# The last two token blocks of a first layer: seven products replaced by plain steps, and the second layer's weight conversion spread over the steps

## The chip, the cores and the metric

The kernel runs on one core of a Trainium2 chip. The metric is the device time of one execution in microseconds. The engines have queues of their own that work in order: PE multiplies matrices, ACT (ScalarE) and DVE (VectorE) work elementwise, POOL (GpSimd) too, and SP issues nearly all DMA transfers. The traces put all operations that go through the kernel's ordering helper on its line 62, so rows are told apart by tile names.

## The reference, cut to what matters

Chunked attention (4 batches, 8 heads, 768 positions, 64 per head, 8 memory keys) gives 3072 tokens of 512 values. Two layers follow:

```python
h = x @ w_in                                  # 3072 x 512 @ 512 x 2048
g = np.maximum(h, 0.0) + np.log1p(np.exp(-np.abs(h)))     # first layer: softplus
y = g @ w_out                                 # 2048 x 512
h = y @ w_in2
g = np.maximum(h, 0.0) + alpha * np.minimum(h, 0.0)       # second layer
out = g @ w_out2
```

Each fp32 operand is split into a high and a low part that PE can multiply at full speed, and a product of two operands is three matmuls: high by high, high by low, low by high.

## The kernel before

**Tokens and hidden units.** The tokens are 6 blocks of 512 (`NB`), the hidden units 16 strips of 128 (`NF`). A plain step (`pe_h` L408, `act_first` L421, `high`/`low` L429 and L434, `pe_out` L469) takes one block and one strip: 12 matmuls of 128x512 from the resident weights `W[f]` into a PSUM bank (`ps_hh`), softplus and split on ACT and DVE (`ta`, `g`), and 12 matmuls into the four sums of the block (`ps_o`). `SEGMENTS` (L43) lists the steps: blocks 0 and 1 in alternating pieces, then blocks 2 and 3 whole, 64 steps (`NPLAIN` = 4).

**Pairs.** Blocks 4 and 5 of the first layer, and all six of the second, go through in pairs with fewer multiplications: `quad` (L575) computes two strips for both blocks of a pair by seven products of 6 matmuls each (`ps_q`), where steps would take 48 matmuls in the same place, from seven combinations of the weights and seven of the activations. Eight quads make a pair, and `pairs` (L637) runs them and then the rest of the output sums. The first product of a quad is copied by ACT (`tc<-ps_q`). `PAIRS` (L45) is one pair of the first layer, then three of the second. A pair's operands are streamed from DRAM: `in_ops` holds the weight combinations in eight groups (one for each quad), `out_ops` the output weights, each already split. The activations come from `y_dram`, and for the first layer's pair from `x_dram`, to which attention stores blocks 4 and 5 (`a_high` L375).

**Weights.** The inputs arrive as float64 words. `load_raw` (L170) loads 128x512 of them, `convert_a` and `convert_b` (L176, L191) turn them into fp32 with five DVE instructions (`word`), and for the second layer each group of four such halves then takes: the sums on POOL (`weight_sums` L232, tile `wsum`), and six stagings, each a high part cast by ACT (`high_to`, `wst`), a low part subtracted by POOL and a store issued by SP (`low_to` L224). The raw words, the sums and the stagings share three buffers (`raw` in the plan), the words two.

**Order.** Before anything is issued, `Plan.run` (L91) walks through the pieces that `add` registered (engine, reckoned us, due time, what they come after, buffers taken and given) and writes them out in the order in which they would start; that is then the order of every in-order queue. Pieces without an engine stand for transfers, with a reckoned duration. Attention's 24 tiles are pieces of this plan with due times between the steps. The sums of the first layer's weights (L754) come first; behind the last of them (`before`, L776) the second layer's conversion begins, with five of the eight groups in the plan (`EARLY`, L775) and three in a list `rest` that `quad` takes piece by piece through `fill` (L613, L618, L625). What remains of `rest` runs at the end of the first pair's quads (L649).

**The seam.** `switch_pools` (L484) gives attention's buffers to the activations of the pairs, `load_y`, `sum_y` and `split_y` make the operands of the first pair, and buffers of `W` become free as the last block's steps finish (`w` in the plan). The last output sums of the steps are issued inside the first quad.

Of the kernel before, what the change touches and what calls it, by code (L numbers as in the profile page):

```python
# [135 lines left out]
def attention_mlp_mlp_kernel(ctx: ExitStack, tc, qk, v, w1, w2, consts, out):  # L136
# [26 lines left out]
    x_dram = dpool.tile([DM, NTOK - NPLAIN * N2], F32, name="x_dram")  # L163
    in_ops = [dpool.tile([NQ, P, 2, 7, HK], F32, name=f"in_ops{n}") for n in range(2)]
    out_ops = [dpool.tile([NQ, P, 2, 2, DM], F32, name=f"out_ops{n}") for n in range(2)]
# [62 lines left out]
    def split_to(src, n, to):  # L228

        low_to(src, n, high_to(src, n), to)  # L230

    def weight_sums(layer, q):  # L232
        if layer:
            m0, m1 = words[1, 4 * q], words[1, 4 * q + 2]
        else:
            m = rpool.tile([P, 2, DM], F32, tag="raw", name="wboth")
            for e in range(2):
                w = W[2 * q + e].bitcast(F32)
                nc.gpsimd.tensor_tensor(out=m[:, e, :], in0=w[:, 0, :DM], in1=w[:, 1, :DM], op=ALU.add)
            m0, m1 = m[:, 0, :], m[:, 1, :]  # L240
        t = rpool.tile([P, 4, HK], F32, tag="raw", name="wsum")
# [5 lines left out]
        sums[layer, q] = t  # L247

    def split_sums(layer, q, n):
        split_to(sums[layer, q][:, n:n + 2, :], DM, in_ops[layer][q][:, :, S1 + n:S1 + n + 2, :])  # L250
        if n:
            sums.pop((layer, q))

    def store_plain(q):

        for e in range(2):
            w = W[2 * q + e].bitcast(F32)
            if e == 0:
                nc.sync.dma_start(out=in_ops[0][q][:, :, A11:A12 + 1, :], in_=w[:, :, :DM].rearrange("p a (k n) -> p a k n", k=2))
            else:  # L260
                nc.sync.dma_start(out=in_ops[0][q][:, :, A22, :], in_=w[:, :, HK:DM])
            nc.sync.dma_start(out=out_ops[0][q][:, e], in_=w[:, :, DM:])

    def split_plain(q):
        split_to(words.pop((1, 4 * q)), DM, in_ops[1][q][:, :, A11:A12 + 1, :])
        split_to(words.pop((1, 4 * q + 2))[:, HK:], HK, in_ops[1][q][:, :, A22, :])

    def split_out(f):
        split_to(words.pop((1, 2 * f + 1)), DM, out_ops[1][f // 2][:, f % 2])
# [105 lines left out]
    def a_high(t):  # L375
        room, (b, c) = st[t][0], divmod(t, TB)
        if b < NPLAIN:
            n = slice(c * QT, (c + 1) * QT)
            for e, x in enumerate(x_of(b)):
                act.copy(out=x[:, 0, :, n], in_=x_ps[t][:, 2 * e:2 * e + 2, :])  # L380
        else:
# [109 lines left out]
    def load_y(p, h):  # L491

        layer, pair = PAIRS[p]
        src, first = (y_dram, 0) if layer else (x_dram, NPLAIN)
        for key, kc, b in ((B11, h, 0), (T1, h, 1), (B21, h + 2, 0), (B22, h + 2, 1)):
            t = y_raw[p, h, key] = raw_y("yraw")
            tok = (2 * pair + b - first) * N2
            nc.sync.dma_start(out=t, in_=src[kc * P:(kc + 1) * P, tok:tok + N2])
# [27 lines left out]
    def load_w_in(n):  # L526
        if n >= len(PAIRS) * NQ:
            return
        p, q = divmod(n, NQ)
        for a, b in ((0, 4), (4, 7)):  # L530
            t = wpool.tile([P, 2, b - a, HK], F32R, tag="w", name="win")
            nc.sync.dma_start(out=t.bitcast(F32), in_=in_ops[PAIRS[p][0]][q][:, :, a:b, :])
# [3 lines left out]
    def load_w_out(n):  # L536
        if n >= 2 * len(PAIRS) * NQ:
# [3 lines left out]
        nc.sync.dma_start(out=t.bitcast(F32), in_=out_ops[PAIRS[p][0]][q % NQ])  # L541
# [13 lines left out]
    def activate(layer, src, f, to):  # L555
        if not layer:
            act.activation(out=to, in_=src, func=AF.Softplus)
            return
# [4 lines left out]
    def out2(p, b, f):  # L563
        n = (2 * p + b) * NQ + f // 2
        layer, pair = PAIRS[p]
        if f == 0:
            acc[p, b] = acc_banks()
        out_sums(acc[p, b], layer, g2.pop((p, b, f)), w_out[n][:, f % 2], f == 0, f == NF - 1)
# [3 lines left out]
        if f == NF - 1:  # L572
            drain(acc.pop((p, b)), layer, 2 * pair + b)

    def quad(p, q, between, fill):  # L575
        n, layer = p * NQ + q, PAIRS[p][0]
# [29 lines left out]
        activate(layer, x1, f0, a0)  # L606
# [6 lines left out]
        fill()  # L613
        product(p, n, A22, T4, x3, False)
        activate(layer, stash[p, f1], f1, stash[p, f1])
        a1 = tpool.tile([P, N2], F32, tag="ta", name="ta", bufs=2)
        activate(layer, x3, f1, a1)
        fill()  # L618
# [18 lines left out]
    def pairs(between, rest):  # L637
        def fill():
            if rest:
                rest.pop(0)()  # L640

        for p in range(len(PAIRS)):
            for q in range(NQ):
                quad(p, q, between, fill)
# [4 lines left out]
            while rest:  # L649
                fill()  # L650
# [58 lines left out]

    def tile(t, prev, due):  # L710
# [10 lines left out]
        for u in range(2):  # L721
            add(("s", t, u), "PE", 0.5, due - 13, lambda u=u: a_scores(t, u), [("qk", t)] + ([("s", t, 0)] if u else [("s", prev, 1)] if prev >= 0 else []) + ([("m", t - 2, u)] if start and t > 1 else [("t", TB - 1, 1)] if t == TB else []),
# [8 lines left out]
        to_dram = t >= NPLAIN * TB  # L731
        for u in range(2):
            add(("t", t, u), "PE", 0.45, due - 5, lambda u=u: a_transpose(t, u), [("n", t)], ["pa"], ["s"] if u and few and not to_dram else [])
            add(("pt", t, u), "ACT", 0.58, due - 4, lambda u=u: a_turned(t, u), [("t", t, u)], [("tb", "tl")[u]], ["pa"])
        free_x = {2: [("ds", 23)], 3: [("ds", 31)]}.get(t // TB, [])
        add(("v*", t), "PE", 0.9, due - 3, lambda: a_values(t), [("pt", t, 0), ("pt", t, 1), ("v", t)], ["h" if start else "pa"], ["tb", "tl"] + (["v"] if few else []))
        if to_dram:
            add(("xh", t), "ACT", 0.6, due - 2, lambda: a_high(t), [("v*", t)], [], ["pa"])
            add(("xl", t), "", 4.0, due, lambda: None, [("xh", t)], [], ["s"])
        else:  # L740
            add(("xh", t), "ACT", 0.75, due - 2, lambda: a_high(t), [("v*", t)] + free_x)
            add(("xl", t), "DVE", 0.84, due - 1, lambda: a_low(t), [("xh", t)], [], ["h" if start else "pa"])
# [11 lines left out]
    for q in range(NQ):  # L754
        due = when[23 + 15 * q // 8] + 20
        add(("sums", q), "POOL", 6.6, due, lambda q=q: (store_plain(q), weight_sums(0, q)),
            [("wl", 4 * q + k) for k in range(4)] + [("raw", 2 * NF - 1)] + ([("sl", q - 1, 2)] if q else []), ["raw", "raw"], ["raw"])
        for n in (0, 2):
            def high_piece(q=q, n=n):
                staged[q, n] = high_to(sums[0, q][:, n:n + 2, :], DM)  # L760

            def low_piece(q=q, n=n):
                low_to(sums[0, q][:, n:n + 2, :], DM, staged.pop((q, n)), in_ops[0][q][:, :, S1 + n:S1 + n + 2, :])
            add(("sh", q, n), "ACT", 0.62, due + 3 * n, high_piece, [("sums", q)], ["raw"])
            add(("sl", q, n), "POOL", 1.6, due + 3 * n, low_piece, [("sh", q, n)], [], ["raw"] if n else [])
            add(("ss", q, n), "", 5.0, 0, lambda: None, [("sl", q, n)], [], ["raw"])

    halves = [4 * q + k for q in range(NQ) for k in (0, 2, 1, 3)]

    def weights2(j):  # L770
        convert(1, halves[j])
        if j + 1 < len(halves):
            load_raw(1, halves[j + 1])

    EARLY = 5  # L775
    before = [("sl", NQ - 1, 2)]  # L776
# [136 lines left out]
```

## Time and profile before

| | |
|---|---|
| Median of 3 runs (lowest, highest) | 1256.76 us (1253.38, 1258.38) |
| The profiled execution | 1255.99 us, span of its instructions 1254.2 us |
| PE busy | 1130.6 us, 5760 matmuls |
| DVE, ACT, POOL busy | 735.4, 437.2, 190.6 us |
| Mean granted clock of PE | 0.956 |
| DMA | 263.96 MB, mean 210 GB/s |

The span runs from the first to the last instruction; the execution's own time adds what lies around it. Busy shares are averages over stages with different limits, so the stages are to be read apart: attention start-up (to about 80 us), steps with attention (to 494 us), the first layer's pair (to 758 us), the second layer. The clock is the mean of what was granted to PE, 1.00 being 2.4 GHz and 0.50 being 1.2 GHz.

### The profile page before, as it was taken

To read this page: it belongs to the slowest core of one execution; us is meant where nothing else is said; L and a number is where in the kernel's file an instruction comes from. 1 tells how busy PE (TensorE), PEld (TensorE's weight loads), DVE (VectorE), ACT (ScalarE), POOL (GpSimd) and SP (SyncE) were. 2 spreads that over 40 slices of the span, in tenths; PEclk is the share of its full clock that TensorE was granted. 3 is DMA by queue.
4 is the path that set the end of the run, shared out by engine and by line. 5 is a ranking of instruction groups with operands and counts; after the bars stand their busy time and mean duration, and the time that the engine had idled before them with its cause. 6 is when DMAs were issued, how large, how long until landed. Compare 5 with 4: busy or idle time off the path is not lost.

```text
span 1254.2 us, 15594 instructions
## 1 busy us (share of the span) xinstructions
PE 1130.6 (90%) x5760; PEld 934.4 (74%) x5760; DVE 735.4 (59%) x1488; ACT 437.2 (35%) x810; POOL 190.6 (15%) x180
## 2 busy tenths in 40 slices
PE   6889989999999996054987799999999999999998
PEld 5778878888888785044865588888888888888887
DVE  5889878544567565323552555666656666665542
ACT  5775454554535333122232242111421113311122
POOL 0011214655322213312211100000000000000000
PEclk9999999999999998577998799999999999999999
DMA  9967975645545576473867666446765457554450
GB/s 303 291 221 248 277 226 180 190 118 159 185 138 211 182 269 238 155 241 120 306 241 270 243 227 226 170 172 246 272 245 195 152 196 287 194 225 166 174 225 34
DMA packets 84316, 263.96 MB, mean 210 GB/s; under 512 B 7056, under 2 KB 15248, under 8 KB 76048
## 3 DMA queue, kind: packets, MB, share of 16 engines
q1 hardware_dynamic: 81936, 258.77, 58.6%
q0 software_dynamic: 2304, 4.20, 2.2%
q8 instruction: 45, 0.74, 0.2%
q14 instruction: 31, 0.25, 0.1%
HBM read 197.93 MB, written 65.01 MB: 210 GB/s over the span
## 4 chain that ended last, share of the span: by engine, by line
PE 72%; DMA 13%; DVE 7%; ACT 3%; POOL 2%; issue 2%; SPq 1%; ACTq 0%; DVEq 0%; POOLq 0%
PE ps_o L62 35%; PE ps_q L62 21%; PE ps_hh L62 10%; DMA raw<-in_w_dram 5%; DMA in_ops<-wst 4%; DVE word L62 3%; PE ps_s L62 3%; PE ps_x L62 2%; POOL wst L225 2%; PE ps_t L62 2%; DMA x_dram<-s_sb 1%; DVE s_sb L62 1%; DMA out_ops<-wst 1%; ACT wst L62 1%; DMA y_dram<-o_sb 1%
## 5 line engine op out<-in xcount | busy, mean ns | idle before, releaser
L62 PE MATMUL ps_q<-xop,win 128*128 128x512 f32 x1344 | 325.8, 398 | 83.0 <-ACT tc L62 79.8
L62 PEld LDWEIGHTS ps_q<-xop,win 128*128 128x128 f32 x1344 | 257.9, 192 | 140.2 <-ACT tc L62 81.7
L62 PE MATMUL ps_o<-wout,g 128*128 128x512 f32 x1152 | 268.8, 389 | 0.0
L62 PEld LDWEIGHTS ps_o<-wout,g 128*128 128x128 f32 x1152 | 216.2, 188 | 44.9
L62 PE MATMUL ps_o<-g,wsplit 128*128 128x512 f32 x768 | 191.9, 400 | 5.9 <-DVE g L62 3.6
L62 PE MATMUL ps_hh<-x,wsplit 128*128 128x512 f32 x768 | 189.5, 396 | 1.6 <-ACT x L62 1.2
L62 PEld LDWEIGHTS ps_o<-g,wsplit 128*128 128x128 f32 x768 | 145.0, 192 | 37.3 <-DVE g L62 4.5
L62 PEld LDWEIGHTS ps_hh<-x,wsplit 128*128 128x128 f32 x768 | 143.2, 190 | 31.9 <-ACT x L62 1.4
L62 DVE TENSOR_TENSOR g<-ta,g 128x512 fp32r<-128x512 f32 x128 | 102.3, 799 | 72.8 <-ACT g L62 69.2
L62 ACT CAST g<-ta 128x512 fp32r<-128x512 f32 x128 | 79.6, 622 | 110.8 <-DVE ta L62 105.8
L62 ACT COPY tc<-ps_q 128x512 f32<-128x512 f32 x64 | 37.6, 587 | 210.3 <-PE ps_q L62 204.2
L62 PE MATMUL ps_o<-g,wout 128*128 128x512 f32 x384 | 92.4, 396 | 3.7 <-ACT o_sb L62 2.8
L62 DVE SCALAR_TENSOR_TENSOR word<-raw,word 128x512 int32<-128x512 int32 x128 | 92.7, 725 | 3.8
L62 DVE TENSOR_TENSOR g<-gb,g 128x512 fp32r<-128x512 f32 x64 | 45.0, 703 | 77.4 <-ACT g L62 76.9
L62 PEld LDWEIGHTS ps_o<-g,wout 128*128 128x128 f32 x384 | 73.7, 192 | 20.3 <-ACT o_sb L62 3.2
L62 DVE TENSOR_TENSOR u<-ps_q,tc 128x512 f32<-128x512 f32 x32 | 22.1, 691 | 94.0 <-PE ps_q L62 69.1
L62 ACT CAST g<-gb 128x512 fp32r<-128x512 f32 x64 | 39.9, 623 | 102.4 <-PE ps_o L62 102.2
L62 ACT ACTIVATE ta<-ps_hh 128x512 f32<-128x512 f32 x64 | 38.3, 598 | 95.0 <-PE ps_hh L62 94.9
L62 DVE TENSOR_SCALAR word<-raw 128x512 int32<-128x512 int32 x64 | 34.4, 538 | 55.9 <-DMA raw<-in_w_dram 35.7
L62 PE MATMUL ps_s<-qk 128*128 128x96 f32 x384 | 53.9, 295 | 10.9 <-DMA qk<-in_qk_dram 6.1
L62 DVE TENSOR_SCALAR word<-word 128x512 f32<-128x512 f32 (+1 forms) x128 | 60.5, 473 | 4.4
L62 PEld LDWEIGHTS ps_s<-qk 128*128 128x128 f32 x384 | 52.2, 210 | 13.6 <-DMA qk<-in_qk_dram 6.4
(62 smaller groups left out, 994.1 us busy)
## 6 DMA issues: line engine op xcount, KB each, us to landing
wout<-out_ops SPq DMA_DIRECT2D x64, 1024.0 KB, 7.1
raw<-in_w_dram SPq DMA_DIRECT2D x64, 512.0 KB, 5.3
win<-in_ops SPq DMA_DIRECT2D x32, 1024.0 KB, 7.0
win<-in_ops SPq DMA_DIRECT2D x32, 768.0 KB, 7.0
in_ops<-wst SPq DMA_DIRECT2D x40, 512.0 KB, 3.2
qk<-in_qk_dram SPq DMA_DIRECT2D x24, 832.0 KB, 6.2
v<-in_v_dram SPq DMA_DIRECT2D x24, 384.0 KB, 5.6
out_ops<-wsplit SPq DMA_DIRECT2D x16, 512.0 KB, 3.9
```

What stands on the lines that cost most here:

```text
L62: i = getattr(self.engine, name)(*args, **kw)
L225: nc.gpsimd.tensor_tensor(out=t[:, 1, :n], in0=src, in1=t[:, 0, :n].bitcast(F32), op=ALU.subtract)
```

## The change

All six blocks of the first layer become plain steps (96 of them), so the first layer's pair goes, with `x_dram`, the first layer's `in_ops` and `out_ops`, the sums of its weights and their stores; `activate` becomes `prelu` on DVE alone. Attention writes the x operand of blocks 2 to 5 into the buffers of blocks that are finished two blocks earlier (`drained`). The second layer's conversion has all eight groups in the plan, begins behind the first layer's last raw load, has due times over steps 24 to 86, and `rest` and `fill` go. The plan's reckoned times change for some pieces: raw loads of the second layer 8 us (5 before), staged stores 6 (5), and attention's work on PE. The operands of the first pair are due by the last steps of the longer list, and the removed functions (`split_sums`, `store_plain`, `split_plain`, `split_out`, `weights2`) have no caller left.

```diff
-NPLAIN = 4
-SEGMENTS = [(b, f0, f1) for f0, f1 in ((0, HALF // 2), (HALF // 2, HALF), (HALF, NF)) for b in range(2)] + [(b, 0, NF) for b in range(2, NPLAIN)]
-PAIRS = [(0, p) for p in range(NPLAIN // 2, NB // 2)] + [(1, p) for p in range(NB // 2)]
+SEGMENTS = [(b, f0, f1) for f0, f1 in ((0, HALF // 2), (HALF // 2, HALF), (HALF, NF)) for b in range(2)] + [(b, 0, NF) for b in range(2, NB)]
+NPAIRS = NB // 2
...
     def a_high(t):
-        room, (b, c) = st[t][0], divmod(t, TB)
-        if b < NPLAIN:
-            n = slice(c * QT, (c + 1) * QT)
-            for e, x in enumerate(x_of(b)):
-                act.copy(out=x[:, 0, :, n], in_=x_ps[t][:, 2 * e:2 * e + 2, :])
-        else:
-            o = room[:, :DM].rearrange("p (k n) -> p k n", k=KD)
-            act.copy(out=o, in_=x_ps.pop(t))
-            tok = t * QT - NPLAIN * N2
-            nc.sync.dma_start(out=x_dram.rearrange("(k p) n -> p k n", p=P)[:, :, tok:tok + QT], in_=o)
+        b, c = divmod(t, TB)
+        n = slice(c * QT, (c + 1) * QT)
+        for e, x in enumerate(x_of(b)):
+            act.copy(out=x[:, 0, :, n], in_=x_ps[t][:, 2 * e:2 * e + 2, :])
...
+    drained = [max(i for i in range(len(steps)) if steps[i][0] == b) for b in range(NB)]
...
-        free_x = {2: [("ds", 23)], 3: [("ds", 31)]}.get(t // TB, [])
+        free_x = [("ds", drained[t // TB - 2])] if t >= 2 * TB else []
...
-        + [(16 + c, when[9 + 3 * c] + 10) for c in range(TB)] + [(8 + c, when[22 + 2 * c] + 10) for c in range(TB)]
-        + [(12 + c, when[31 + 3 * c] + 10) for c in range(TB)] + [(20 + c, when[43 + 3 * c] + 10) for c in range(TB)]
+        + [(TB * b + c, when[drained[b - 2] - 2 + (2 if b == 2 else 3) * c] + 10) for b in range(2, NB) for c in range(TB)]
...
-    EARLY = 5
-    before = [("sl", NQ - 1, 2)]
-    add(("raw2", 0), "", 5.0, 0, lambda: load_raw(1, halves[0]), before, ["raw"])
-    for j in range(4 * EARLY):
+    add(("raw2", 0), "", 8.0, 0, lambda: load_raw(1, halves[0]), [("raw", 2 * NF - 1)], ["raw"])
+    for j in range(4 * NQ):
         q, e = divmod(j, 4)
-        k, due = halves[j], when[33 + 28 * j // (4 * EARLY)]
-        add(("cv2", j), "DVE", 2.75, due, lambda j=j: convert(1, halves[j]), [("raw2", j)] + ([("cv2", j - 1)] if j else []), ["word"], ["raw"])
-        add(("raw2", j + 1), "", 5.0, 0, lambda j=j: load_raw(1, halves[j + 1]), [("cv2", j)] + ([("sh2", q - 1, 1, 1)] if 0 else []), ["raw"])
+        k, due = halves[j], when[24 + 64 * j // (4 * NQ)]
+        add(("ca2", j), "DVE", 1.35, due, lambda j=j: convert_a(1, halves[j]), [("raw2", j)] + ([("cv2", j - 1)] if j else []), ["word"])
+        add(("cv2", j), "DVE", 1.42, due, lambda j=j: convert_b(1, halves[j]), [("ca2", j)], [], ["raw"])
+        if j + 1 < 4 * NQ:
+            add(("raw2", j + 1), "", 8.0, 0, lambda j=j: load_raw(1, halves[j + 1]), [("cv2", j)], ["raw"])
...
-            add(("ss2",) + name, "", 5.0, 0, lambda: None, [("sl2",) + name], [], ["raw"])
+            add(("ss2",) + name, "", 6.0, 0, lambda: None, [("sl2",) + name], [], ["raw"])
...
-        due = when[55 + 4 * h]
+        due = when[last - 8 + 4 * h]
...
-    pairs(lambda: pe_out(last), rest)
+    pairs(lambda: pe_out(last))
```

## Rows read from the trace of the kernel before

**Rows 1.** The page, engine totals: busy us, share of the span, instructions.
```profile
PE 1130.6 (90%) x5760; PEld 934.4 (74%) x5760; DVE 735.4 (59%) x1488; ACT 437.2 (35%) x810; POOL 190.6 (15%) x180
```

**Rows 2.** Stages: stretch, length, PE, PEld, DVE, ACT, POOL busy, clock, DMA share, GB/s.
```profile
80.00:331.00 251.00, 246.00 (x1519) 204.57 (x1520) 173.67 (x414) 130.89 (x204) 99.83 (x92) 0.99 0.66 202
331.00:468.00 137.00, 134.25 (x769) 111.24 (x769) 86.75 (x199) 60.82 (x95) 28.13 (x28) 0.99 0.58 202
468.00:494.00 26.00, 20.10 (x77) 15.55 (x76) 15.66 (x22) 10.08 (x18) 7.78 (x7) 0.87 0.75 274
494.00:758.00 264.00, 177.35 (x723) 142.68 (x722) 114.61 (x180) 71.41 (x127) 48.36 (x47) 0.83 0.64 225
758.00:921.00 163.00, 163.00 (x721) 134.97 (x720) 99.39 (x154) 38.13 (x66) 0.00 (x0) 1.00 0.60 219
```

**Rows 3.** Waits of PE from 468 to 758 us: total us, times, longest.
```profile
PE ps_q L62 <- ACT tc L62: 79.8, 4, 48.6
```

**Rows 4.** Timeline of PE about the seam: start, us, operation, idle before it.
```profile
473.82 0.50 PE L62 MATMUL ps_o<-g,wsplit 128*128 128x512 f32 x1 [2.35 <-ACT g L62]
477.07 5.01 PE L62 MATMUL ps_o<-g,wsplit 128*128 128x512 f32 x11 [2.75 <-DVE g L62]
...
493.93 4.24 PE L62 MATMUL ps_q<-xop,win 128*128 128x512 f32 x18
546.78 4.59 PE L62 MATMUL ps_q<-xop,win 128*128 128x512 f32 x12 [48.61 <-ACT tc L62]
```

**Rows 5.** Timeline of ACT: a staging cast amid the steps, and the seam.
```profile
375.38 0.62 ACT L62 CAST wst<-wsum 128x512 fp32r<-128x512 f32 x1 [4.91 <-DMA in_ops<-wst]
...
545.62 0.62 ACT L62 CAST wst<-word 128x512 fp32r<-128x512 f32 x1 [2.43 <-DMA in_ops<-wst]
546.14 0.58 ACT L62 COPY tc<-ps_q 128x512 f32<-128x512 f32 x1
```

**Rows 6.** Chain that ended last, in order of time: start, us, what.
```profile
436.12 2.72 PE ps_hh L62 x12
438.83 2.72 PE ps_o L62 x12
...
757.77 6.80 PE ps_q L62 x30
...
920.98 6.80 PE ps_q L62 x30
```

**Rows 7.** Timeline of POOL: the second layer's sums, and one last staging.
```profile
354.12 0.74 POOL L243 TENSOR_TENSOR wsum<-word 128x256 f32<-128x256 f32 x1 [23.07 <-DVE word L62]
...
382.99 1.39 POOL L225 TENSOR_TENSOR wst<-word,wst 128x512 fp32r<-128x512 f32 x1 [1.80 <-ACT wst L62]
393.18 0.73 POOL L243 TENSOR_TENSOR wsum<-word 128x256 f32<-128x256 f32 x1 [8.80 <-DVE word L62]
...
437.87 0.74 POOL L243 TENSOR_TENSOR wsum<-word 128x256 f32<-128x256 f32 x1 [12.55 <-DVE word L62]
...
490.77 1.06 POOL L243 TENSOR_TENSOR wsum<-word 128x256 f32<-128x256 f32 x1 [8.09 <-DVE word L62]
...
523.32 0.73 POOL L243 TENSOR_TENSOR wsum<-word 128x256 f32<-128x256 f32 x1 [6.70 <-DVE word L62]
```

**Rows 8.** Waits of PE from 80 to 468 us: total us, times, longest.
```profile
PE ps_t L62 <- DVE s_sb L62: 6.4, 3, 3.1
PE ps_hh L62 <- ACT x L62: 0.7, 1, 0.7
```

**Rows 9.** Timeline of SP: last first-layer raw load, first three of the second's.
```profile
192.43 0.47 SPq L173 DMA_DIRECT2D raw<-in_w_dram  x1
...
332.34 2.57 SPq L173 DMA_DIRECT2D raw<-in_w_dram  x3
```

**Rows 10.** DVE's groups, 331 to 494 and 760 to 1250 us: busy, mean ns | idle before.
```profile
L62 DVE TENSOR_TENSOR g<-ta,g 128x512 fp32r<-128x512 f32 x24 | 22.6, 943 | 27.9 <-ACT g L62 27.8
...
L62 DVE TENSOR_TENSOR g<-ta,g 128x512 fp32r<-128x512 f32 x48 | 33.0, 688 | 3.5
```

More of the change, by code (lines that the diff above doesn't have):

```diff
@@ L162, in attention_mlp_mlp_kernel @@
     y_dram = dpool.tile([DM, NTOK], F32, name="y_dram")
-    x_dram = dpool.tile([DM, NTOK - NPLAIN * N2], F32, name="x_dram")
-    in_ops = [dpool.tile([NQ, P, 2, 7, HK], F32, name=f"in_ops{n}") for n in range(2)]
-    out_ops = [dpool.tile([NQ, P, 2, 2, DM], F32, name=f"out_ops{n}") for n in range(2)]
+    in_ops = dpool.tile([NQ, P, 2, 7, HK], F32, name="in_ops")
+    out_ops = dpool.tile([NQ, P, 2, 2, DM], F32, name="out_ops")
     W, raws, words = {}, {}, {}
@@ L226, in low_to, with weight_sums @@
         nc.sync.dma_start(out=to, in_=t[:, :, :n].bitcast(F32))
[L228 to L234, printed above, removed]
-        else:
[L236 to L241, printed above, removed]
+    def weight_sums(q):
+        m0, m1 = words[1, 4 * q], words[1, 4 * q + 2]
+        t = sums[q] = rpool.tile([P, 4, HK], F32, tag="raw", name="wsum")
         sub = dict(op=ALU.subtract)
@@ L246, in weight_sums @@
         nc.gpsimd.tensor_tensor(out=t[:, 3, :], in0=m0[:, HK:], in1=t[:, 1, :], **sub)
[L247 to L269, printed above, removed]
     qk_t, v_t, st, s_room, pt_t = {}, {}, {}, {}, {}
@@ L491, in load_y @@
     def load_y(p, h):
-        layer, pair = PAIRS[p]
-        src, first = (y_dram, 0) if layer else (x_dram, NPLAIN)
         for key, kc, b in ((B11, h, 0), (T1, h, 1), (B21, h + 2, 0), (B22, h + 2, 1)):
             t = y_raw[p, h, key] = raw_y("yraw")
-            tok = (2 * pair + b - first) * N2
-            nc.sync.dma_start(out=t, in_=src[kc * P:(kc + 1) * P, tok:tok + N2])
+            tok = (2 * p + b) * N2
+            nc.sync.dma_start(out=t, in_=y_dram[kc * P:(kc + 1) * P, tok:tok + N2])
     def sum_y(p, h):
@@ L531, in load_w_in @@
             t = wpool.tile([P, 2, b - a, HK], F32R, tag="w", name="win")
-            nc.sync.dma_start(out=t.bitcast(F32), in_=in_ops[PAIRS[p][0]][q][:, :, a:b, :])
+            nc.sync.dma_start(out=t.bitcast(F32), in_=in_ops[q][:, :, a:b, :])
             for k in range(a, b):
@@ L540, in load_w_out @@
         t = wpool.tile([P, 2, 2, DM], F32R, tag="w", name="wout")
-        nc.sync.dma_start(out=t.bitcast(F32), in_=out_ops[PAIRS[p][0]][q % NQ])
+        nc.sync.dma_start(out=t.bitcast(F32), in_=out_ops[q % NQ])
         w_out[n] = t
@@ L553, in product, with prelu @@
                 k += 1
[L555 to L558, printed above, removed]
+    def prelu(src, f, to):
         a = tpool.tile([P, N2], F32, tag="word", name="tp", bufs=2)
@@ L564, in out2 @@
         n = (2 * p + b) * NQ + f // 2
-        layer, pair = PAIRS[p]
         if f == 0:
             acc[p, b] = acc_banks()
-        out_sums(acc[p, b], layer, g2.pop((p, b, f)), w_out[n][:, f % 2], f == 0, f == NF - 1)
+        out_sums(acc[p, b], 1, g2.pop((p, b, f)), w_out[n][:, f % 2], f == 0, f == NF - 1)
         if f % 2:
@@ L572, in out2, with quad @@
         if f == NF - 1:
-            drain(acc.pop((p, b)), layer, 2 * pair + b)
-    def quad(p, q, between, fill):
-        n, layer = p * NQ + q, PAIRS[p][0]
+            drain(acc.pop((p, b)), 1, 2 * p + b)
+    def quad(p, q, between):
+        n = p * NQ + q
         f0, f1 = 2 * q, 2 * q + 1
@@ L605, in quad @@
         a0 = tpool.tile([P, N2], F32, tag="ta", name="ta", bufs=2)
-        activate(layer, x1, f0, a0)
+        prelu(x1, f0, a0)
         x4 = bank(ps_h, "h")
@@ L612, in quad @@
         g2[p, 0, f0] = split(a0)
-        fill()
         product(p, n, A22, T4, x3, False)
-        activate(layer, stash[p, f1], f1, stash[p, f1])
+        prelu(stash[p, f1], f1, stash[p, f1])
         a1 = tpool.tile([P, N2], F32, tag="ta", name="ta", bufs=2)
-        activate(layer, x3, f1, a1)
-        fill()
+        prelu(x3, f1, a1)
         product(p, n, S4, B22, x4, False)
@@ L623, in quad @@
         g2[p, 0, f1] = split(a1)
-        activate(layer, stash[p, f0], f0, stash[p, f0])
-        fill()
+        prelu(stash[p, f0], f0, stash[p, f0])
     def prepare(p):
-        if p >= len(PAIRS):
+        if p >= NPAIRS:
             return []
@@ L635, in prepare, with pairs @@
         return todo
[L637 to L642, printed above, removed]
+    def pairs(between):
+        for p in range(NPAIRS):
             for q in range(NQ):
-                quad(p, q, between, fill)
+                quad(p, q, between)
                 between = lambda p=p, q=q: out2(p, 0, 2 * q + 1)
@@ L730, in tile @@
         add(("n", t), "DVE", 1.4 if by_act(t) == 2 * NPAIR else 1.9 if start else 2.3, due - 7, lambda: a_norm(t), [("e", t)])
-        to_dram = t >= NPLAIN * TB
         for u in range(2):
-            add(("t", t, u), "PE", 0.45, due - 5, lambda u=u: a_transpose(t, u), [("n", t)], ["pa"], ["s"] if u and few and not to_dram else [])
+            add(("t", t, u), "PE", 0.5, due - 5, lambda u=u: a_transpose(t, u), [("n", t)], ["pa"], ["s"] if u and few else [])
             add(("pt", t, u), "ACT", 0.58, due - 4, lambda u=u: a_turned(t, u), [("t", t, u)], [("tb", "tl")[u]], ["pa"])
-        free_x = {2: [("ds", 23)], 3: [("ds", 31)]}.get(t // TB, [])
[L736 to L742, printed above, removed]
+        free_x = [("ds", drained[t // TB - 2])] if t >= 2 * TB else []
+        add(("v*", t), "PE", 1.36, due - 3, lambda: a_values(t), [("pt", t, 0), ("pt", t, 1), ("v", t)], ["h" if start else "pa"], ["tb", "tl"] + (["v"] if few else []))
+        add(("xh", t), "ACT", 0.75, due - 2, lambda: a_high(t), [("v*", t)] + free_x)
+        add(("xl", t), "DVE", 0.84, due - 1, lambda: a_low(t), [("xh", t)], [], ["h" if start else "pa"])
     prev = -1
@@ L791, in split_task @@
             add(("sl2",) + name, "POOL", us, due + 5, low_piece, [("sh2",) + name], [], give)
-            add(("ss2",) + name, "", 5.0, 0, lambda: None, [("sl2",) + name], [], ["raw"])
+            add(("ss2",) + name, "", 6.0, 0, lambda: None, [("sl2",) + name], [], ["raw"])
         if e == 1:
-            add(("sums2", q), "POOL", 3.4, due + 3, lambda q=q: weight_sums(1, q), [("cv2", j)], ["raw"])
-            split_task((q, 0), lambda q=q: words[1, 4 * q], DM, in_ops[1][q][:, :, A11:A12 + 1, :], [("sums2", q)], 1.6, ["word"])
-            split_task((q, 1), lambda q=q: words[1, 4 * q + 2][:, HK:], HK, in_ops[1][q][:, :, A22, :], [("sl2", q, 0)], 0.9, ["word"])
+            add(("sums2", q), "POOL", 3.4, due + 3, lambda q=q: weight_sums(q), [("cv2", j)], ["raw"])
+            split_task((q, 0), lambda q=q: words[1, 4 * q], DM, in_ops[q][:, :, A11:A12 + 1, :], [("sums2", q)], 1.6, ["word"])
+            split_task((q, 1), lambda q=q: words[1, 4 * q + 2][:, HK:], HK, in_ops[q][:, :, A22, :], [("sl2", q, 0)], 0.9, ["word"])
             for n in (0, 2):
-                split_task((q, 2 + n), lambda q=q, n=n: sums[1, q][:, n:n + 2, :], DM, in_ops[1][q][:, :, S1 + n:S1 + n + 2, :],
+                split_task((q, 2 + n), lambda q=q, n=n: sums[q][:, n:n + 2, :], DM, in_ops[q][:, :, S1 + n:S1 + n + 2, :],
                            [("sl2", q, 1 + n)], 1.6, ["raw"] if n else [])
```

41 lines of the change are left out of this document (6 added, 35 removed).

## The prediction

> **What bounds the kernel now.** I read the page's engine totals first, then the same engines by stage, then the waits and the timeline of PE at the seams, and last the queues that feed the stage that stands still.
>
> The totals show PE busy 1130.6 of 1254.2 us, with DVE next at 735.4 [rows 1]. That alone says "PE-bound", with some 124 us lost somewhere. The stages say where [rows 2]. From 80 to 468 us, the plain steps with attention beside them, PE is idle 5.0 and 2.75 us. From 758 us on it is not idle at all. Between 494 and 758 us, where the first layer's blocks 4 and 5 go through seven products, PE is busy 177.35 of 264 us at a mean granted clock of 0.83, that is, part of the time at the lower of its two levels. Four waits, all put down to ACT's copy of a product, hold 79.8 us of that [rows 3]; the first lasts 48.61 us, and the matmuls behind it run slowly, twelve in 4.59 us [rows 4]. ACT was not busy: its copy at 546.14 us stands in its queue right behind a staging cast of the second layer's weights that waited for a store to free a buffer [rows 5]. So the stall belongs to the weight conversion, which PE gets to only because ACT works in order. The same pair of blocks without conversions takes 163.2 us (757.77 to 920.98 us in rows 6, one layer on).
>
> **The sum.** Three terms, against this execution.
>
> First, what goes out: from the first product at 493.93 us [rows 4] to the first product of the second layer at 757.77 us [rows 6], 263.8 us. The second layer then follows as it does now, so everything behind 757.77 us is kept.
>
> Second, what comes in: 2 blocks of 16 steps, each 12 matmuls into the hidden bank and 12 into the sums, at 2.72 us each [rows 6], 5.44 us a step and 174.1 us for 32. By count it is 48 matmuls more than the products needed (8 groups of hidden units, 48 for 42 in each), so against an undisturbed pair the change alone costs 10.9 us. The gain is the stall, not the arithmetic.
>
> Third, the last steps before the seam: at 473.82 and 477.07 us PE waits 2.35 and 2.75 us, and 11 matmuls then take 5.01 us, 2.5 more than at 2.72 for twelve [rows 4]. These 7.6 us come from staging and from the operands of the first products being made in the same stretch. The second cause stays, the first should be gone. Bounds 0 and 7.6; I take 4.
>
> Span: 1254.2 - 263.8 + 174.1 - 4 = 1160.5 us. The execution's own time is 1255.99, 1.8 over its span, and the median of the runs 0.8 over that: **1163 us**.
>
> **What I cost at nothing.** The attention tiles of blocks 4 and 5 keep their PE work. Each trades one copy and a store for two casts on ACT and two subtractions on DVE, which are busy 60.82 and 86.75 of 137 us beside the steps [rows 2]; without that cover I estimate it by the larger split of rows 10: 2 x 0.69 us of DVE a tile, 11 us for 8 tiles. Their results now need a buffer of a finished block; the nearest row is PE's wait for such a cast, 0.7 us in one case [rows 8], so 0 to 3 for four blocks. The first layer's weight sums, POOL's own, fall away with their stores, the loads of the products' weights and the round trip of the activations: off the path, no gain until PE waits for them. On SP, 32 loads and 48 stores of the conversion now pass ahead of later loads of q, k and v, and a store that waits for POOL holds those. The nearest row is PE's wait for what attention's transposes read, 6.4 us in all over 388 us that hold the stores of the first layer's sums and of two eighths of the second's [rows 8]; it is in the steps already, so I add 0, bound 0 to 6. Less DVE work falls beside blocks 0 and 1, where a tile of block 4 ran; at most PE's idle time from 80 to 331 us, 5.0, comes back.
>
> **Does the conversion fit?** This decides. I follow the weights in eighths, one for each group of the products. The sums of an eighth begin at 354.12, 393.18, 437.87 and 490.77 us beside the steps, so 45.6 us apart on the mean and 52.9 at worst; 32.6 us once PE stands still [rows 7]. It starts at 332.34 us now, held back by the first layer's sums, though the first layer's last raw load was at 192.43 us [rows 9]. After the change it may follow that load: first sums at 192.4 + (354.1 - 332.3) = 214 us, the eighth at 214 + 7 x 45.6 = 533, done some 30 us later (354.12 to 384.38 for the first), at 564. The steps end at 493.9 + 174.1 - 4 = 664 us. But the plan that writes the order now reckons a load at 8 us for 5, and an eighth has four in series: at most 12 us more, 57.6 each, done at 647. So 17 to 100 us to spare, and from 60 us an eighth on something sticks out.
>
> **A rule against it.** DVE's subtraction that splits a step's result takes 943 ns from 331 to 494 us, beside POOL's conversion, and 688 ns in the second layer, where POOL is idle [rows 10]. The change puts POOL's subtractions beside nearly all remaining steps.
>
> The Trainium skill, "SBUF — State Buffer", section "Who interferes with whom", says that a VectorE instruction with two SBUF inputs and a GpSimd instruction that reads SBUF exclude each other, the later one waiting the other out. The two means agree with that; by the rule alone every step would be slower.
>
> In the trace PE does not pass it on: its waits from 80 to 468 us fall in four groups, the two largest of them in rows 8, and none is for that subtraction. I therefore cost it at 0, and keep the other end: 0.255 us on each of some 74 steps, 19 us.
>
> **Rivals.**
> *Tail.* The plan puts the last eighth behind the last steps, as it does now with its fifth, and the first product waits behind its staging on ACT. For it: the longer planned loads, and the pace that worsened from 39.1 to 52.9 us. Against: the margin above. One eighth alone is 32.6 us [rows 7]: 1163 + 33 = 1196 us; two would be 1228.
> *Shared port.* The 19 us above reach PE: 1182 us. Against it stands rows 8.
> *Slower: staging holds ACT.* All 48 stagings now stand in ACT's queue among the steps' activations, and a cast that waits for a store to land holds the softplus behind it, so the next step's sums. The longest such wait amid running steps is 4.91 us [rows 5]; if all 48 cost PE that, 236 us, 1399 in all. It decides from 100 / 48 = 2.1 us each, where 1263 us is reached. Against: PE's whole idle time in the 137 us that held the stagings of two eighths and a half, six each, is 2.75 us [rows 2], 0.2 for each.
> *No change in what matters.* If the plan still left the conversion to the end, three eighths behind the last step, at 3 x 32.6 = 98 us, would bring back today's time. With the first load allowed 140 us earlier I give this no chance of its own; it is the tail's far end.
>
> **How the numbers follow.** The forecast 0.72, the port 0.07, the tail 0.17, staging on ACT 0.04 (half of it beyond the point where it is slower). What a measurement of this kernel can tell from no change is about 0.5%, 6 us. The first three cases all lie 28 us or more below that, but for a tail of three eighths. So faster 0.97, same 0.01, slower 0.02. Low end: 1163 - 3.6 (rest of the third term) - 5.0 - 2.75 (all idle time beside steps) - 2.5 (spread of the runs, half of 1253 to 1258) = 1149. High end: the tail with one eighth and that spread, 1199. It leaves out a tail of two eighths and staging, under 0.1, and as much again for what I didn't think of.
>
> **What would show it.** Right: PE busy about 25 of 25 us in every slice from 80 us on; last hidden product of a plain step near 660 us; granted clock 0.97 to 1.00 after the first 80 us; no wait of several us at the first product; POOL's last subtraction before that; the sums of the eighths 45 to 58 us apart, the first near 214 us. The second layer from its first product to the end 496 us, as now. Wrong: sums more than 60 us apart or POOL busy behind the last step (tail); PE waits on DVE's split spread evenly over steps 24 to 95 (port); PE waits on ACT's activations, with ACT waiting for stores (staging). A first load of the second layer's weights long after 200 us would break the fit itself.

## The result and the profile after

The changed kernel takes 1153.2 us (median of 4 runs, 1151.2 to 1153.9) where the kernel before takes 1257.5 beside it: a ratio of 0.917, 95% interval 0.915 to 0.920. The profiled execution is 1152.67 us with a span of 1150.8. Forecast were 1163 us, 1149 to 1199.

The engine totals of the page, which answer to [rows 1]:

```profile
PE 1125.5 (98%) x5808; PEld 935.4 (81%) x5808; DVE 695.7 (60%) x1450; ACT 408.9 (36%) x770; POOL 121.1 (11%) x116
```

PE has 48 matmuls more and is busy 5 us less, in a span 103 us shorter: it was never its own work that was to be saved. At 2.72 us for twelve, 48 matmuls are 10.9 us, so by this estimate some 16 us of busy time went with the stretches at the lower clock. POOL lost 69.5 us with the first layer's sums and their stagings.

The stages, with the columns of [rows 2]; the first layer now ends at 654 us:

```profile
80.00:331.00 251.00, 246.85 (x1434) 204.83 (x1435) 182.28 (x411) 114.30 (x189) 53.86 (x51) 0.99 0.53 153
331.00:468.00 137.00, 137.00 (x797) 114.23 (x796) 71.87 (x187) 60.57 (x97) 28.27 (x27) 1.00 0.46 152
468.00:494.00 26.00, 26.00 (x162) 21.91 (x161) 16.55 (x57) 13.20 (x21) 5.02 (x6) 1.00 0.50 171
494.00:640.00 146.00, 146.00 (x714) 120.97 (x713) 77.28 (x130) 55.88 (x96) 28.66 (x25) 1.00 0.49 167
640.00:655.00 15.00, 15.00 (x68) 12.43 (x67) 2.08 (x3) 3.66 (x6) 0.00 (x0) 1.00 0.36 130
655.00:818.00 163.00, 163.00 (x721) 134.97 (x720) 99.36 (x154) 38.13 (x66) 0.00 (x0) 1.00 0.60 215
```

From 331 us on there is no idle time of PE in any of these stretches, the granted clock is 1.00 throughout, and POOL is done before the seam. The 264 us at a clock of 0.83 of [rows 2] have no counterpart.

The timeline of PE at the seam, which answers to [rows 4]: the first product follows the last sums of the steps without a wait.

```profile
648.77 2.88 PE L61 MATMUL ps_hh<-x,wsplit 128*128 128x512 f32 x12
651.49 2.88 PE L61 MATMUL ps_o<-g,wsplit 128*128 128x512 f32 x12
654.21 6.96 PE L61 MATMUL ps_q<-xop,win 128*128 128x512 f32 x30
661.01 2.88 PE L61 MATMUL ps_o<-g,wsplit 128*128 128x512 f32 x12
```

The timeline of POOL, which answers to [rows 7]: the first, second and last eighth's sums, and the last two stagings.

```profile
210.58 1.26 POOL L226 TENSOR_TENSOR wsum<-word 128x256 f32<-128x256 f32 x1
...
275.29 0.73 POOL L226 TENSOR_TENSOR wsum<-word 128x256 f32<-128x256 f32 x1 [2.14 <-DVE word L61]
...
585.82 1.07 POOL L226 TENSOR_TENSOR wsum<-word 128x256 f32<-128x256 f32 x1 [12.60 <-DVE word L61]
...
613.86 3.42 POOL L219 TENSOR_TENSOR wst<-word,wst 128x512 fp32r<-128x512 f32 x2 [1.19 <-ACT wst L61]
```

The sums stand (585.82 - 210.58) / 7 = 53.6 us apart, and the conversion is done at 617.3 us, 37 us ahead of the first product.

What ACT's staging casts waited for between 180 and 654 us (total us, times, longest), first before, then after:

```profile
ACT wst L62 <- DMA in_ops<-wst: 51.2, 15, 8.2
ACT wst L62 <- DVE word L62: 30.6, 8, 8.1
```

```profile
ACT wst L61 <- DVE word L61: 3.5, 2, 2.1
ACT wst L61 <- DMA in_ops<-wst: 1.6, 2, 1.1
```

These are the waits that stood in ACT's queue ahead of the copies for PE. The two together went from 82 us to 5.

### The profile page after: what moved, and what is told of

It reads as the page before. It is cut to its first block, busy times and chain, and to the rows that moved or that the text cites. A ratio compares the mean times of both kernels' runs of the same rounds, so it can differ in the third digit from the quotient of the medians.

```text
span 1150.8 us, 15268 instructions
## 1 busy us (share of the span) xinstructions
PE 1125.5 (98%) x5808; PEld 935.4 (81%) x5808; DVE 695.7 (60%) x1450; ACT 408.9 (36%) x770; POOL 121.1 (11%) x116
## 4 chain that ended last, share of the span: by engine, by line
PE 95%; DVE 2%; DMA 1%; issue 1%; ACT 0%; SPq 0%; DVEq 0%; ACTq 0%
PE ps_o L61 46%; PE ps_hh L61 23%; PE ps_q L61 20%; PE ps_s L61 3%; PE ps_x L61 2%; PE ps_t L61 2%; DMA qk<-in_qk_dram 1%; DVE word L61 1%; DVE v L61 1%; DVE x L61 0%; ACT pt L61 0%; DVE sm L61 0%; DVE o_sb L61 0%; DVE r L61 0%; SPq L239 0%
## 5 line engine op out<-in xcount | busy, mean ns | idle before, releaser
L61 PE MATMUL ps_hh<-x,wsplit 128*128 128x512 f32 x1152 | 283.3, 395 | 2.3 <-DVE x L61 1.3
L61 PE MATMUL ps_o<-g,wsplit 128*128 128x512 f32 x1152 | 282.4, 394 | 1.8 <-DVE g L61 1.8
L61 PEld LDWEIGHTS ps_hh<-x,wsplit 128*128 128x128 f32 x1152 | 216.0, 190 | 48.0 <-DVE x L61 2.0
L61 PEld LDWEIGHTS ps_o<-g,wsplit 128*128 128x128 f32 x1152 | 215.9, 189 | 47.0 <-DVE g L61 2.3
L61 PE MATMUL ps_q<-xop,win 128*128 128x512 f32 x1008 | 236.3, 389 | 0.0
L61 PEld LDWEIGHTS ps_q<-xop,win 128*128 128x128 f32 x1008 | 189.2, 188 | 39.3
L61 ACT ACTIVATE ta<-ps_hh 128x512 f32<-128x512 f32 x96 | 57.4, 598 | 217.2 <-PE ps_hh L61 217.0
L61 DVE TENSOR_TENSOR g<-gb,g 128x512 fp32r<-128x512 f32 x48 | 33.2, 692 | 60.4 <-ACT g L61 60.0
L61 DVE TENSOR_SCALAR tp<-ps_q,cst 128x512 f32<-128x512 f32 x48 | 36.0, 750 | 38.0 <-PE ps_q L61 38.0
L61 ACT ACT_TABLE_LOAD x40 | 51.3, 1283 | 1.4 <-PEq L813 0.7
L219 POOL TENSOR_TENSOR wst<-word,wst 128x512 fp32r<-128x512 f32 (+1 forms) x32 | 39.0, 1221 | 112.5 <-ACT wst L61 112.5
```

What stands on the lines that cost most here:

```text
L61: i = getattr(self.engine, name)(*args, **kw)
L219: nc.gpsimd.tensor_tensor(out=t[:, 1, :n], in0=src, in1=t[:, 0, :n].bitcast(F32), op=ALU.subtract)
```

## The experiments

The changed kernel was run twice more as a control beside the others: 1152.6 and 1152.3 us, expected as 

> The changed kernel itself, to be compared with the three runs beside it on the same chip: 1153 us within 3 us by every theory.

 and 

> The changed kernel itself once more, beside the next three on the same chip: 1153 us within 3 us by every theory.

**Without the second layer's conversion** (in the kernel before). This takes away the suspected cause and keeps the products; the second layer then works with the first layer's operands, of the same sizes, so the version serves for its time alone.

```diff
-            nc.sync.dma_start(out=t.bitcast(F32), in_=in_ops[PAIRS[p][0]][q][:, :, a:b, :])
+            nc.sync.dma_start(out=t.bitcast(F32), in_=in_ops[0][q][:, :, a:b, :])
...
-        nc.sync.dma_start(out=t.bitcast(F32), in_=out_ops[PAIRS[p][0]][q % NQ])
+        nc.sync.dma_start(out=t.bitcast(F32), in_=out_ops[0][q % NQ])
...
-    EARLY = 5
+    EARLY = 0
...
-    add(("raw2", 0), "", 5.0, 0, lambda: load_raw(1, halves[0]), before, ["raw"])
...
-    for q in range(EARLY, NQ):
+    for q in range(0):
```

> The kernel before without the second layer's weight conversion: its 32 loads, DVE conversions, POOL sums, stagings and stores are left out, and the second layer streams the first layer's prepared operands in their place (same sizes). Theory (the stall between 494 and 758 us is the conversion alone, waited for through ACT's queue): the first layer's pair takes the 163.2 us of an undisturbed pair and the last steps lose nothing, so 1257.5 - 100.6 - 7.6 = 1149 us (1144 to 1156), below the changed kernel by up to the 10.9 us that products save over steps. Rival (the pair is slow for reasons of its own, its operand loads or the round trip of the activations): most of the 100 us stays, 1200 us or more.

Measured: 1141.6 us, ratio 0.909 (0.905 to 0.914). Its stages, and the timeline of PE at the two ends of the first layer's pair:

```profile
331.00:468.00 137.00, 135.81 (x781) 112.69 (x781) 53.06 (x144) 57.09 (x89) 0.00 (x0) 1.00 0.35 122
468.00:494.00 26.00, 26.00 (x116) 21.53 (x115) 6.31 (x10) 8.87 (x15) 0.00 (x0) 1.00 0.50 165
494.00:645.00 151.00, 151.00 (x668) 125.04 (x667) 54.79 (x84) 52.48 (x89) 0.00 (x0) 1.00 0.60 220
```

```profile
481.39 6.96 PE L62 MATMUL ps_q<-xop,win 128*128 128x512 f32 x30
```

```profile
644.60 6.96 PE L62 MATMUL ps_q<-xop,win 128*128 128x512 f32 x30
```

The pair takes 644.60 - 481.39 = 163.2 us, as an undisturbed pair (920.98 - 757.77). All of the 100 us of stall was the conversion; which of its parts held PE this run does not say, for that stand [rows 5] and the next run. The time lies 2.4 us under the range that I had expected (1144 to 1156), because the seam also comes 12.5 us earlier than in [rows 4], where I had reckoned 7.6. Not all of the 12.5 is the conversion's: PE's idle time to 331 us is 1.2 us less too, and the kernel before began the second layer's conversion only at 332 us. Against the changed kernel the products are faster by 9.6 us in span (1141.2 for 1150.8) and 11.6 in the medians, beside 10.9 us for 48 matmuls at 2.72 us for twelve.

**All of the conversion in the plan** (in the kernel before, without the early start): what the second half of the change does by itself when no time is made for it.

```diff
-    EARLY = 5
+    EARLY = NQ
...
-        add(("raw2", j + 1), "", 5.0, 0, lambda j=j: load_raw(1, halves[j + 1]), [("cv2", j)] + ([("sh2", q - 1, 1, 1)] if 0 else []), ["raw"])
+        if j + 1 < 4 * NQ:
+            add(("raw2", j + 1), "", 5.0, 0, lambda j=j: load_raw(1, halves[j + 1]), [("cv2", j)], ["raw"])
```

> The kernel before with all eight eighths of the conversion in the plan, none taken by the quads; still behind the first layer's sums and with the old dues. Theory (an eighth that is not done by the last step costs its isolated 32.6 us at the seam): three more eighths at the seam, 98 us, and the 52 us of stalls inside the pair go: 1257.5 + 98 - 52 = 1303 us (1285 to 1320). Rival (it is the planning as such that helps, pieces in the quads being badly placed): 1257 us or less.

Measured: 1296.4 us, ratio 1.032 (1.027 to 1.037). That is inside the expected range. One wait of PE has nearly all of it, and POOL's sums show four eighths in a row behind the steps, which end near 496 us:

```profile
PE ps_q L62 <- ACT tc L62: 138.3, 1, 138.3
```

```profile
525.90 0.72 POOL L243 TENSOR_TENSOR wsum<-word 128x256 f32<-128x256 f32 x1 [6.55 <-DVE word L62]
557.13 0.72 POOL L243 TENSOR_TENSOR wsum<-word 128x256 f32<-128x256 f32 x1 [6.70 <-DVE word L62]
588.50 0.72 POOL L243 TENSOR_TENSOR wsum<-word 128x256 f32<-128x256 f32 x1 [6.72 <-DVE word L62]
619.86 0.72 POOL L243 TENSOR_TENSOR wsum<-word 128x256 f32<-128x256 f32 x1 [6.80 <-DVE word L62]
```

They are 31.3 us apart. So planning the conversion without earlier room for it makes the kernel slower; what does not fit is paid at the seam, an eighth at a time.

**A later start** (in the changed kernel), at step 30 and at step 40. The second is near the first half of the change alone, since the kernel before began its conversion there.

```diff
-    add(("raw2", 0), "", 8.0, 0, lambda: load_raw(1, halves[0]), [("raw", 2 * NF - 1)], ["raw"])
+    add(("raw2", 0), "", 8.0, 0, lambda: load_raw(1, halves[0]), [("raw", 2 * NF - 1), ("h", 30)], ["raw"])
```

(and 40 in place of 30.) 

> The changed kernel with the second layer's first raw load held until step 30's hidden product, about 250 us for 179. Theory (a margin of 37 us between the last staging at 617 us and the first product at 654 us; what sticks out runs at 32.6 us an eighth instead of 53.6): 72 - 37 = 35 us late, 35 x 32.6 / 53.6 = 21 us, 1174 us (1160 to 1190). Rival (where the conversion starts is of no matter once the steps cover it, the plan catches up): 1153 us.

> The same, held until step 40's hidden product, about 322 us, near the 332 us at which the conversion begins in the kernel before. Theory: 143 - 37 = 106 us late, 106 x 0.61 = 65 us, 1218 us (1195 to 1250). Rival (no matter): 1153 us. This is also the first half of the change, steps for products, nearly without the second.

Measured: 1154.9 us from step 30, 1197.5 us from step 40 (ratios 0.920 and 0.953); the second is inside its expected range. The edit did not quite do what I meant: SP issued the first three loads as early as in the changed kernel (at 179.9, 187.4 and 193.5 us from step 30, for 178.6, 186.1 and 192.2), since nothing ties them to step 30, and it was DVE's conversions, in DVE's order, that began late, at 257 and 329 us for 193. POOL's first sums, last sums and last staging from step 30, and PE's first product:

```profile
272.47 1.11 POOL L226 TENSOR_TENSOR wsum<-word 128x256 f32<-128x256 f32 x1
...
631.30 0.74 POOL L226 TENSOR_TENSOR wsum<-word 128x256 f32<-128x256 f32 x1 [18.67 <-DVE word L61]
...
656.77 2.54 POOL L219 TENSOR_TENSOR wst<-word,wst 128x512 fp32r<-128x512 f32 x2
```

```profile
656.19 6.96 PE L61 MATMUL ps_q<-xop,win 128*128 128x512 f32 x30
```

The first product comes at 656.19 us, without a wait: the last staging ends 3 us behind it and nobody minds. 64 us of delay cost 2 us, not 21, and the time lies outside the range that I expected (1160 to 1190). The 37 us that I read as margin were too few, for the eighths drew together to (631.30 - 272.47) / 7 = 51.3 us. From step 40 the last two sums, and the wait of PE:

```profile
650.41 1.06 POOL L226 TENSOR_TENSOR wsum<-word 128x256 f32<-128x256 f32 x1 [13.63 <-DVE word L61]
682.85 0.72 POOL L226 TENSOR_TENSOR wsum<-word 128x256 f32<-128x256 f32 x1 [3.81 <-DMA out_ops<-wst]
```

```profile
PE ps_q L61 <- ACT tc L61: 41.7, 1, 41.7
```

Here the stall is back, in the same place and form as before. Between the two, conversions 72 us later cost 42.6 us more, 0.59 of it; the isolated pace over the pace beside the steps, 32.6 / 53.6, had predicted 0.61. That is one pair of runs and no law, since the pace beside the steps was not 53.6 us here either: the last eighth alone stood at the seam. So the rival fell too: the start does matter, once the slack of some 64 us is used up. Steps for products, with the whole conversion in the plan and starting where it did, bring about 60 of the 104 us, and the earlier start the other 45. The other order, the seven products kept and the conversion begun earlier, was not run; how much of the gain it would have brought stays open.

**Subtractions on POOL twice, and four times** (in the changed kernel), to see whether POOL's work beside DVE reaches PE. The edit for four times; for twice the line stands twice.

```diff
-        nc.gpsimd.tensor_tensor(out=t[:, 1, :n], in0=src, in1=t[:, 0, :n].bitcast(F32), op=ALU.subtract)
+        for _ in range(4):
+            nc.gpsimd.tensor_tensor(out=t[:, 1, :n], in0=src, in1=t[:, 0, :n].bitcast(F32), op=ALU.subtract)
```

> The changed kernel with each of the conversion's 48 low-part subtractions on POOL done twice, some 58 us more of POOL beside the steps. Theory (DVE has the slack to wait POOL out, PE does not see it): within 3 us of the changed kernel. Rival (shared port: what DVE's split loses to POOL reaches PE): DVE's splits of the steps lengthen and PE waits for them, 5 us or more slower.

> The changed kernel with each of the conversion's 48 subtractions on POOL done four times, some 175 us more of POOL beside the steps; twice gave 4 us more in the median with overlapping intervals and 1 us in the profile. Theory (DVE has the slack): the chain of an eighth lengthens by 6 x 3 x 1.2 = 22 us on the chip, so it may reach behind the last step, which shows as one wait of the first product; without that within 4 us of the changed kernel, and PE's waits on DVE's split below 4 us in all between 180 and 640 us. Rival (shared port): 12 us or more, spread over the steps as waits on DVE's split.

Measured: twice, 1156.6 us, ratio 0.920 (0.918 to 0.922) for the control's 0.917 (0.916 to 0.919), intervals that overlap: unclear. Four times, 1212.6 us, ratio 0.967: 60 us slower, and my expectation of 4 us fell. It is no tail, for POOL ended at 689 us and the first product came at 717 us without a wait:

```profile
678.37 10.19 POOL L220 TENSOR_TENSOR wst<-word,wst 128x512 fp32r<-128x512 f32 x7
```

```profile
716.92 6.96 PE L61 MATMUL ps_q<-xop,win 128*128 128x512 f32 x30
```

The two largest waits of PE from 180 to 645 us (36 us in all there, 0.5 in the control), and the waits of DVE and ACT for POOL from 180 to 654 us:

```profile
PE ps_t L61 <- DVE s_sb L61: 16.5, 6, 5.5
PE ps_o L61 <- DVE g L61: 9.3, 5, 3.8
```

```profile
DVE word L61 <- POOL wst L220: 32.9, 8, 6.6
```

```profile
ACT wst L61 <- POOL wst L220: 29.2, 7, 6.2
```

In the changed kernel the last two are 1.2 and 3.0 us. A conversion on DVE waits for POOL to free one of the two word buffers, and behind it in DVE's queue stand attention's normalising and the splits of the steps, for which PE waits. That is the coupling of the seam once more, through another engine; but it is not shown to be the whole. Of the 62.7 us by which the span grew, PE was idle for 38.3, and its 5808 matmuls were busy 24.4 us longer, in stretches whose granted clock fell below 1.00, such as this:

```profile
331.00:468.00 137.00, 125.33 (x710) 103.13 (x710) 81.35 (x166) 51.18 (x83) 75.82 (x64) 0.96 0.40 136
```

The split itself, in the changed kernel and with POOL four times, from 180 to 640 us:

```profile
L61 DVE TENSOR_TENSOR g<-ta,g 128x512 fp32r<-128x512 f32 x73 | 55.4, 759 | 127.4 <-ACT g L61 127.3
```

```profile
L61 DVE TENSOR_TENSOR g<-ta,g 128x512 fp32r<-128x512 f32 x63 | 55.5, 882 | 96.0 <-ACT g L61 95.9
```

It grew by 123 ns, 8 us over 63 of them. The Trainium skill, "SBUF — State Buffer", section "Who interferes with whom", gives a rule by which a DVE instruction with two SBUF inputs contends with a GpSimd instruction that reads SBUF. The trace agrees: the 32 splits that overlap no POOL instruction take 686 ns, the 31 that do 1085. The conversions' instructions grew as well, and all 1450 instructions of DVE together were busy 55.5 us longer (751.2 for 695.7), which is not small beside the waits. How much of the 60 us is the lengthened DVE instructions and how much the waits in the queues was not separated, so my rival of that run is not refuted; a run with POOL's extra work outside the chain of the buffers would tell and wasn't tried.

**Stores twice** (in the changed kernel), so that staging buffers come free later than planned: the test of the rival that was to make the kernel slower.

```diff
         nc.sync.dma_start(out=to, in_=t[:, :, :n].bitcast(F32))
+        nc.sync.dma_start(out=to, in_=t[:, :, :n].bitcast(F32))
```

> The changed kernel with each of the 48 staged stores issued twice to the same place, so that a staging buffer comes free some 3 us later than the plan reckoned. Theory (ACT's queue is what couples the conversion to PE, with 1.6 us of such waits in the changed kernel): ACT's waits for stores rise to some 50 to 150 us in all, but a step leaves ACT about 4 us of slack, so PE loses 0 to 15 us, and any loss is PE waiting on ACT's activations or casts. Rival of the prediction (each wait of a staging cast is a loss of PE, and the kernel would be slower than before from 2.1 us each): near 3 us each, 100 us or more.

Measured: 1157.0 us, ratio 0.923 (0.921 to 0.925), 4.7 us above the control beside it. The waits of ACT, and the largest of PE on ACT's activations, from 180 us on:

```profile
ACT wst L61 <- DMA in_ops<-wst: 36.5, 15, 5.9
```

```profile
PE ps_hh L61 <- ACT ta L61: 1.5, 1, 1.5
```

ACT waited 35 us more, less than the 50 to 150 us that I had expected, and the kernel lost at most 5, with intervals that just touch: 0.1 us for each of the 48 stagings, where 2.1 would have been needed.

**The old reckoned times** in the plan (in the changed kernel; timed twice).

```diff
-            add(("s", t, u), "PE", 0.58, due - 13, lambda u=u: a_scores(t, u), [("qk", t)] + ([("s", t, 0)] if u else [("s", prev, 1)] if prev >= 0 else []) + ([("m", t - 2, u)] if start and t > 1 else [("t", TB - 1, 1)] if t == TB else []),
+            add(("s", t, u), "PE", 0.5, due - 13, lambda u=u: a_scores(t, u), [("qk", t)] + ([("s", t, 0)] if u else [("s", prev, 1)] if prev >= 0 else []) + ([("m", t - 2, u)] if start and t > 1 else [("t", TB - 1, 1)] if t == TB else []),
...
-            add(("t", t, u), "PE", 0.5, due - 5, lambda u=u: a_transpose(t, u), [("n", t)], ["pa"], ["s"] if u and few else [])
+            add(("t", t, u), "PE", 0.45, due - 5, lambda u=u: a_transpose(t, u), [("n", t)], ["pa"], ["s"] if u and few else [])
...
-        add(("v*", t), "PE", 1.36, due - 3, lambda: a_values(t), [("pt", t, 0), ("pt", t, 1), ("v", t)], ["h" if start else "pa"], ["tb", "tl"] + (["v"] if few else []))
+        add(("v*", t), "PE", 0.9, due - 3, lambda: a_values(t), [("pt", t, 0), ("pt", t, 1), ("v", t)], ["h" if start else "pa"], ["tb", "tl"] + (["v"] if few else []))
...
-    add(("raw2", 0), "", 8.0, 0, lambda: load_raw(1, halves[0]), [("raw", 2 * NF - 1)], ["raw"])
+    add(("raw2", 0), "", 5.0, 0, lambda: load_raw(1, halves[0]), [("raw", 2 * NF - 1)], ["raw"])
...
-            add(("raw2", j + 1), "", 8.0, 0, lambda j=j: load_raw(1, halves[j + 1]), [("cv2", j)], ["raw"])
+            add(("raw2", j + 1), "", 5.0, 0, lambda j=j: load_raw(1, halves[j + 1]), [("cv2", j)], ["raw"])
...
-            add(("ss2",) + name, "", 6.0, 0, lambda: None, [("sl2",) + name], [], ["raw"])
+            add(("ss2",) + name, "", 5.0, 0, lambda: None, [("sl2",) + name], [], ["raw"])
```

> The changed kernel with the plan's old reckoned times (second layer's raw loads 5 us, staged stores 5, attention's PE pieces 0.5, 0.45 and 0.9). Theory (the reckoned loads set the pace of the eighths, 53.6 us now; shorter ones bring it to about 46 with more margin, and PE is full either way): within 3 us of the changed kernel, sums of the eighths 43 to 49 us apart. Rival (the longer reckonings keep ACT and SP from waiting for transfers): PE waits between 180 and 650 us of 5 us or more.

> The version with the old reckoned times once more, which gave 1150.3 us for 1152.6: if the gain is real, 1 to 4 us below the changed kernel beside it; if not, within 1 us.

Measured: 1150.3 us and then 1152.0, beside controls of 1152.6 and 1152.3. The first looked like a gain, the second shows none. The sums came 49.7 us apart, just outside the 43 to 49 that I expected, and ACT waited 1.4 us for stores: this part of the change does nothing to the time that can be measured.

**Low parts on POOL at the start** (in the changed kernel), an attempt at the idle 17 us of the first 80.

```diff
-        eng = (dve, nc.gpsimd)[k % 2]
-        add(("wl", k), ("DVE", "POOL")[k % 2], (0.69, 1.6)[k % 2], need - 1, lambda k=k, eng=eng: low_w(k, eng), [("wh", k)], [], ["word"])
+        onpool = k % 2 or n < 16
+        eng = nc.gpsimd if onpool else dve
+        add(("wl", k), "POOL" if onpool else "DVE", 1.6 if onpool else 0.69, need - 1, lambda k=k, eng=eng: low_w(k, eng), [("wh", k)], [], ["word"])
```

> The changed kernel with the low parts of the first 16 halves of the first layer's weights all on POOL (half of them on DVE now), to take 8 x 0.69 us off DVE in the first 110 us, where DVE is busy 60 of 80 us and PE idle 17. Theory (DVE's order sets the start of the steps): 0 to 5 us faster. Rival (POOL's 1.3 to 2 us for one, and the port, delay the weights that the next step waits for): 0 to 5 us slower.

Measured: 1155.2 us, ratio 0.920 (0.918 to 0.922), 2.6 us above the control with overlapping intervals: no gain, and perhaps a small loss. PE's idle time in the first 80 us hardly moved, 16.5 us for 17. No run beat the changed kernel by a measurable amount with the whole computation in it.

## Why the prediction was right, step by step

**The stall and its cause.** Right, and shown: without the conversion the pair takes 163.2 us; with all of it in the plan and no earlier start, four eighths fall behind the steps and the stall is one wait of 138.3 us; started at step 40 in the changed kernel it returns.

**First and second term.** What follows the first product of the second layer was kept to 0.1 us: 1150.8 - 654.4 = 496.4 us, as 1254.2 - 757.8 (654.4 is its start in the chain that ended last, as in [rows 6]; the timeline has 654.21). The 10.9 us for the steps fit the 9.6 to 11.6 us between the changed kernel and the one without conversion.

**Third term.** This is where the 10 us between 1163 and 1153 lie. The first product was to come at 664 us and came at 654.4. I took 4 of 7.6 us for the last steps, because the operands of the first products are still made there, and all 7.6 came back: that work cost PE nothing here. I also left PE's idle time beside the earlier steps standing: the 2.75 us from 331 to 468 us went to none, and the 5.0 from 80 to 331 us to 4.15. That is 7.2 of the 9.6. Most of the rest stands in the first 80 us, where PE is idle 17.0 us for 19.2; the controls have 17.2 and 18.7 there, so that the change caused it is not shown. The run without conversion agrees: its PE is idle 1.2 us for 2.75 from 331 to 468 us, so the conversion cost a little ahead of 468 us as well, and the third term was undersized.

**Does it fit.** Right, with some luck in the parts. First sums were forecast at 214 us and measured at 210.6, but by two misses that nearly cancel. The first load came at 178.62 us and not behind 192.4, since the first layer's last raw load was itself earlier (173.7 us); from it to the sums 32 us passed and not 21.8.

```profile
178.62 0.33 SPq L171 DMA_DIRECT2D raw<-in_w_dram  x1
```

The pace was forecast between 45.6 and 57.6 us and measured 53.6. Here too the parts are off: with the old reckoned times it is 49.7, so the longer reckonings made 4 us and not up to 12, and the other 4 over 45.6 I had not counted. Ready was to be between 564 and 647 us; measured 617. What I read from it was too cautious, as step 30 showed: the pace is not fixed, and a late conversion closes up before anything sticks out.

**What was costed at nothing.** It was: from 180 us to the end this is all that PE waits in the control, and in the changed kernel's own profile.

```profile
PE ps_s L61 <- ACT pt L61: 0.5, 2, 0.2
```

That holds for this load of POOL and no more, as the run with four subtractions shows.

**Rivals.** The tail's mechanism and its price are real (31 to 32 us an eighth behind the steps), but the margin kept it away. The port did not reach PE here. Staging on ACT costs 0.1 us each even with stores doubled, so the slower end was far off. The lengthening of DVE's split is there all the same, but smaller than I priced it: 759 ns in the mean where [rows 10] has 943. It is not that fewer splits meet POOL's work. From 331 to 494 us 12 of 24 overlap a POOL instruction before and 13 of 25 after; those that do take 1198 ns before and 848 after, the others 689 and 687. So each meeting became shorter; why is not shown.

## What to carry to other kernels

Count the stall before the arithmetic: a form with more matmuls won 104 us here, because the form with fewer had left the weight conversion no time to hide. Background work on in-order queues cost nearly nothing here while it was early (0.5 us of waits), and its isolated length behind the last step that covered it; compare its pace and its start with the end of its cover, and expect some slack in the pace. A wait for a buffer on an in-order engine is paid by whatever stands behind it, so look for the one that is short of buffers (ACT for staging at the seam; perhaps DVE for words, where lengthened instructions may weigh as much) as well as for the engine that is busy.

## What the runs showed that was not expected

Doubling POOL's subtractions cost at most 4 us and quadrupling them 60: there is an edge between the two. Whether it lies where POOL's chain for one eighth no longer fits between DVE's conversions, or where DVE's own lengthened work fills its slack, the runs don't tell. And the first loads of a conversion that the plan holds back still went out at once, three of them, as many as there are buffers, and the fourth at 283 us: the planned order binds each queue by itself, not one queue to another.
